# Decode attention with a partly kept K cache: keys dealt to partitions in runs of 64, K and V loaded in whole, half or quarter heads

## The chip, the cores and the metric

The kernel runs on one core of a Trainium2 chip. The metric is the device time of one execution in microseconds (us), from the runs listed below. The profile is one execution, recorded instruction by instruction; its span runs from the first instruction to the last. PE is TensorE, DVE is VectorE, ACT is ScalarE, POOL is GpSimd, SP is the engine whose queue issues the transfers. MiB are powers of two, MB and GB are powers of ten.

## The reference

Two identical rounds of decode attention and a small MLP, with one new token for each of 8 batch rows. The K and V caches are the same in both rounds.

```python
B, Sq, D = 8, 1, 512
Hq, Hkv, Sk, Dh = 32, 8, 8192, 128        # k_cache, v_cache: [8, 8, 8192, 128] bf16
F = 1792
...
q = (x @ wq).reshape(B, Sq, Hq, Dh).transpose(0, 2, 1, 3)
k = jnp.repeat(k_cache, 4, axis=1); v = jnp.repeat(v_cache, 4, axis=1)
p = _softmax(jnp.einsum("bhqd,bhkd->bhqk", q, k) * Dh ** -0.5)
o = jnp.einsum("bhqk,bhkd->bhqd", p, v) ... @ wo
...
x = x + _A_ref(_layernorm(x), A_k_cache, A_v_cache, A_wq, A_wo)
x = x + _B_ref(_layernorm(x), B_w1, B_w2)     # silu(x @ w1) @ w2
x = x + _A_ref(_layernorm(x), A_k_cache, A_v_cache, A_wq, A_wo)
x = x + _B_ref(_layernorm(x), B_w1, B_w2)
```

One K or V head of one batch row is 8192 x 128 bf16, 2 MiB. There are 64 K heads and 64 V heads, and each is wanted twice.

## The kernel before

**Tasks and positions.** The work is cut into 128 tasks: (layer, batch row, KV head). Each task has GPT = 8 groups of 1024 keys, so there are 1024 positions p, one for each iteration of the main loop (line 738). At position p the kernel emits, in this order: transposes of K up to position p + LT = p + 2 (`emit_t`, line 421), for every second position the scores of two groups (`emit_s`, line 459), and the P.V matmuls of position p - LP = p - 14 (`emit_pv`, line 523). Softmax steps of the task before, and one step of the "chain" (output projection, layer norms, MLP and next query of one batch row), are put in between. At the end of the iteration, `issue_until(p)` (line 391) issues the loads that are free to go.

**Transposes.** K arrives with keys on partitions. A group is transposed by 8 PE matmuls against the identity into PSUM (line 430), and copied back over the same place in SBUF by ACT (line 436) or DVE (line 438). V is used as it arrives.

**The arena.** K and V live in one SBUF arena of NSLOT = 27 slots of 4 KB per partition (512 KB each). Four slots hold one head. A slot is loaded by one DMA on SP's queue: key (k, p, c) of the head goes to partition p, so that a quarter head is one contiguous stretch of 512 KB in DRAM and each partition's row has 4 KB.

**What is kept.** For heads g = 3 to 7 (20 of the 32 quarters of a batch row) K, once transposed, stays in the arena from layer 0 until layer 1 of the same batch row has used it. So 88 tasks load K and V, and 40 tasks load V alone and have no transposes.

**The order of tasks** (`make_tasks`, line 138). For each batch row come, in turn:
- the *filling stage*: five layer-0 tasks with g = 3 to 7, whose K stays, so that the free part of the arena shrinks from 27 slots to 7;
- the *narrow stage*: five or six tasks with g = 0 to 2, of layer 1 of the row before and layer 0 of later rows, which run through the 7 slots left; the chain of the batch row is worked off here, and what is left of it is run at once before layer 1 begins;
- the *V-only stage*: five layer-1 tasks with g = 3 to 7, which give back the 20 slots.

The first row has three more full tasks in front, and the last three tasks stand at the end.

**The order of loads** (`plan_loads`, line 169). It works ahead of time, on positions. Each load has a position at which it is needed (`need`: K two positions before its task's group, V 14 after) and one after which its slot is free again. Loads are sorted by need; each takes the slot that came free first, and `after` is the position that freed it. At run time `issue_until(p)` issues from the front of this list while `after <= p`; a load whose `after` is larger holds back all loads behind it. The issue itself (`issue`, line 349) makes SP wait for the last readers of the slot.

```python
            def issue_until(pos):
                while queue and queue[0].after <= pos:
                    issue(queue.pop(0))
```

**The start.** Four K quarters are issued, then wq (4 MiB, rows of 8 KB), then every load with `after = -2`, which is one for each slot left, then wo, w1 and w2 (7.86 MB; rows of 1 KB, 3.5 KB and 1 KB), all on SP's queue.

Of the kernel before, what the change touches and what calls it, by code (L numbers as in the profile page):

```python
# [12 lines left out]
GRP = 8  # L13
GPT = 8
GPG = 2
NSLOT = 27
KEEP = 20
LT = 2
PRE = 10
LP = 14  # L20
EARLY = 4
# [5 lines left out]
KB = 512  # L27
QUAD = 32
FAR = 1e38
PVN = 12  # L30
# [4 lines left out]
BF16 = mybir.dt.bfloat16  # L35
# [91 lines left out]
class Load:  # L127


    __slots__ = ("kind", "b", "g", "k", "need", "free", "slot", "after")  # L130

    def __init__(self, kind, b, g, k, need, free):
        self.kind, self.b, self.g, self.k = kind, b, g, k
        self.need, self.free = need, free
        self.slot, self.after = None, None

# [31 lines left out]

def plan_loads(tasks, kept, nslot, ngran):

    at = {t: i for i, t in enumerate(tasks)}
    loads = []
    for i, (layer, b, g) in enumerate(tasks):
        for k in range(ngran):
            i0 = i * GPT + k * GPG
            if layer == 0 or (g, k) not in kept:
                need = -1 if i0 < PRE else i0 - LT
                last = i if layer or (g, k) not in kept else at[(1, b, g)]
                loads.append(Load("K", b, g, k, need, last * GPT + (k + 1) * GPG - 1))
            loads.append(Load("V", b, g, k, i0 + GPG - 1 + LP, i0 + GPG - 1 + LP))  # L180
    loads.sort(key=lambda d: (d.need, d.kind))
    free = [(-2, s) for s in range(nslot)]
    for d in loads:
        free.sort()
        d.after, d.slot = free.pop(0)
        assert d.after < d.need or d.need == -1 and d.after == -2, (d.kind, d.need, d.after)
        free.append((d.free, d.slot))
    return loads
# [18 lines left out]
def _build(ctx, nc, A_x, A_k_cache, A_v_cache, A_wq, A_wo, B_w1, B_w2, out):  # L207
# [8 lines left out]
    NGRAN = NCH // (GRP * GPG)  # L216
    SLOT = GRP * GPG * 128
    assert GPT * GRP == NCH and NGRAN * GPG == GPT and KT * 128 == D and FT * 128 == F

    order = [(g, k) for g in range(HKV) for k in range(NGRAN)]  # L220
    kept = set(order[len(order) - KEEP:])
    tasks = make_tasks(B, HKV, (len(order) - KEEP) // NGRAN)
    assert len(tasks) == 2 * B * HKV
    task_at = {t: i for i, t in enumerate(tasks)}
    loads = plan_loads(tasks, kept, NSLOT, NGRAN)
    NG = len(tasks) * GPT

# [16 lines left out]

    ARENA = sb([128, NSLOT * SLOT], BF16, "arena")

    def chunk(slot, c):
        o = slot * SLOT + c * 128
        return ARENA[:, o:o + 128]

    def half(slot, h):
        o = slot * SLOT + h * GRP * 128
        return ARENA[:, o:o + GRP * 128]

# [47 lines left out]
    syn = Sync(nc, ctx)  # L302
    slsem = [DmaCounter(syn.new_sem(f"sl{i}")) for i in range(NSLOT)]
    wsem = {n: DmaCounter(syn.new_sem(f"w_{n}")) for n in ("wq", "wo", "w1", "w2", "x")}
# [8 lines left out]

    def r_half(slot, h):
        return res(f"slot{slot}_{h}")

# [28 lines left out]

    k_slot = {}
    v_slot = {}

    def issue(d):
        cache = A_k_cache if d.kind == "K" else A_v_cache  # L350
        src = cache[d.b, d.g].rearrange("(k p c) d -> k p (c d)", k=NGRAN, p=128)[d.k]
        dst = ARENA[:, d.slot * SLOT:(d.slot + 1) * SLOT]
        dma(sp, dst, src, slsem[d.slot], writes=[r_half(d.slot, 0), r_half(d.slot, 1)])
        (k_slot if d.kind == "K" else v_slot)[(d.b, d.g, d.k)] = d.slot

    with nc.Block() as block:

        @block.sync
        def _(sync_eng):
# [42 lines left out]

            for _n in range(NGRAN):
                issue(queue.pop(0))
# [8 lines left out]
            def has_t(i):  # L413
                layer, _b, g = tasks[i // GPT]
                return layer == 0 or (g, (i % GPT) // GPG) not in kept

            def where(i):
                _l, b, g = tasks[i // GPT]
                return b, g, (i % GPT) // GPG, i % GPG

            def emit_t(i):
                b, g, k, h = where(i)
                slot = k_slot[(b, g, k)]
                n = tevacs[0]
                tevacs[0] += 1
                tb = evacs[0] % NTP
                evacs[0] += 1
                tpv = TPp[tb][:, :].rearrange("p (k q) -> p k q", q=128)
                steps = [
                    lambda c=c: pe.transpose(tpv[:, c, :], chunk(slot, h * GRP + c), ident[:, :])  # L430
                    for c in range(GRP)
                ]
                mm_group(steps, reads=[r_half(slot, h), "ident"], writes=[f"TP{tb}"])
                dst = half(slot, h)
                if n % 8 in ACT_EVAC:
                    op(act, lambda: act.copy(dst, TPp[tb][:, :]), reads=[f"TP{tb}"], writes=[r_half(slot, h)])  # L436
                else:
                    op(dve, lambda: dve.tensor_copy(dst, TPp[tb][:, :]), reads=[f"TP{tb}"], writes=[r_half(slot, h)])  # L438

# [15 lines left out]
            def emit_s(i):  # L455
                ti = i // GPT
                b, g, k, _h = where(i)
                slot = k_slot[(b, g, k)]
                bank, qn = ti % NSCP, ti % NQB
                steps = [  # L460
                    lambda c=c: pe.matmul(  # L461
                        SCp[bank][c * QUAD:(c + 1) * QUAD, :], QB[qn][:, NGRAN - 1 - k:NGRAN - 1 - k + QUAD],
                        ARENA[:, slot * SLOT + c * KB:slot * SLOT + (c + 1) * KB],
                        start=(k == 0), stop=(k == NGRAN - 1),
                    )
                    for c in range(NQ)
                ]
                mm_group(steps, reads=[r_half(slot, 0), r_half(slot, 1), f"QB{qn}"], writes=[f"SC{bank}"])

# [53 lines left out]
            def emit_pv(i):  # L523
                ti = i // GPT
                b, g, k, h = where(i)
                slot = v_slot[(b, g, k)]
                ob, pb = ti % 2, ti % NPT
                pv = PT[pb][:, :, :].rearrange("p x (c r k) -> p x c k r", c=NQ, k=NGRAN)
                otp = OTp[ob][:, 0:REP * PVN].rearrange("p (r n) -> p r n", n=PVN)
                steps = []  # L530
                for c in range(GRP):
                    cc = (i % GPT) * GRP + c
                    steps.append(
                        lambda c=c, cc=cc: pe.matmul(  # L534
                            otp, chunk(slot, h * GRP + c), pv[:, cc % CPB, cc // CPB % NQ, k, :].unsqueeze(2).to_broadcast([128, REP, PVN]),
                            start=(cc == 0), stop=(cc == NCH - 1),
                        )
                    )
                mm_group(steps, reads=[r_half(slot, h), f"PT{pb}"], writes=[f"OT{ob}"])

# [286 lines left out]
```

## Time and profile before

| | |
|---|---|
| runs | 1214.28, 1216.26, 1218.24 us; median 1216.26 |
| span of the profiled execution | 1216.1 us |
| PE busy | 1048.9 us (86%) |
| DVE, ACT, POOL busy | 598.4, 373.9, 70.3 us |
| DMA | 468.02 MB, mean 385 GB/s |
| K loads, V loads | 352 and 512, 512 KB each, median 14.9 and 10.8 us from issue to landing |
| mean granted PE clock | 0.967 |

The profiled execution's own time is not listed apart from its span; the span lies 0.2 us under the median of the runs. On the page, "DMA" gives the busy share of the 16 DMA engines in 40 equal slices of the span, in tenths, and "GB/s" what they moved in each slice. A line of the waits names the engine that waited, for whom, the total, the number of waits and the longest. In a view by stretch, each line has the busy time of each engine, the granted PE clock, the DMA share and GB/s.

### The profile page before, as it was taken

Reading aid. Unit: us, or ns where it says so; the run is one execution under the profiler, and the core shown is the slowest. Engines: PE = TensorE matmul, PEld = TensorE weight load, DVE = VectorE, ACT = ScalarE, POOL = GpSimd, SP = SyncE. Lnnn points to the kernel's source line nnn. Section 1 sums busy time; section 2 is a strip of 40 time slices with the busy share of each in tenths; the row PEclk is TensorE's granted clock in tenths of the full one; section 3 lists DMA queues with packets and bytes.
Section 4 is the critical chain, followed back from the end, with each engine's and each line's share of the span. In section 5 each row is a group of like instructions: output and inputs, shape, how many; then the busy total and the mean of one; then the engine's idle time right before and its main releaser. Section 6 shows DMA issues by size and latency. Waiting matters only on the chain.

```text
span 1216.1 us, 45620 instructions
## 1 busy us (share of the span) xinstructions
PE 1048.9 (86%) x19960; PEld 787.6 (65%) x19960; DVE 598.4 (49%) x1833; ACT 373.9 (31%) x658; POOL 70.3 (6%) x172
## 2 busy tenths in 40 slices
PE   2798888888988889889998898888988898899995
PEld 2576675667666676667676676667666666667664
DVE  2454554546445554546345654556354554456443
ACT  1233322333133322333133322332233322333231
POOL 0000000000000000000000000000000000000000
PEclk9889999999999899999879999999999999999896
DMA  9999989999999999999999999999999999999994
GB/s 373 385 397 402 393 328 409 408 400 389 365 408 409 355 343 403 408 400 388 390 408 403 383 369 409 408 399 362 376 407 402 389 370 408 408 392 380 394 407 169
DMA packets 131621, 468.02 MB, mean 385 GB/s; under 512 B 13904, under 2 KB 19808, under 8 KB 130912
## 3 DMA queue, kind: packets, MB, share of 16 engines
q1 hardware_dynamic: 131424, 465.12, 98.3%
q8 instruction: 158, 2.59, 0.8%
q14 instruction: 39, 0.32, 0.1%
HBM read 465.05 MB, written 0.01 MB: 382 GB/s over the span
## 4 chain that ended last, share of the span: by engine, by line
DMA 53%; PE 34%; SPq 5%; DVE 5%; issue 2%; POOLq 0%; POOL 0%; ACT 0%; DVEq 0%
DMA arena<-in_A_k_cache_dram 46%; PE OTp L534 11%; PE TPp L430 10%; PE SCp L461 5%; SPq L331 5%; DMA arena<-in_A_v_cache_dram 5%; PE MISC L603 4%; DMA wo<-in_A_wo_dram 2%; DVE arena L438 1%; PE OTp L482 1%; PE MISC L621 1%; PE TPp L510 1%; DVE PT L514 0%; DVE tr L585 0%; DVE yr L588 0%
## 5 line engine op out<-in xcount | busy, mean ns | idle before, releaser
L430 PE MATMUL TPp<-ident,arena 128*128 128x128 bf16 x5632 | 403.5, 223 | 80.2 <-DMA arena<-in_A_k_cache_dram 64.6
L436 ACT COPY arena<-TPp 128x1024 bf16<-128x1024 bf16 x264 | 267.2, 1012 | 603.8 <-PE TPp L430 603.8
L438 DVE COPY arena<-TPp 128x1024 bf16<-128x1024 bf16 x440 | 302.0, 688 | 279.4 <-PE TPp L430 279.1
L534 PE MATMUL OTp<-PT,arena 128*128 128x48 bf16 x8192 | 387.2, 186 | 48.1 <-DMA arena<-in_A_v_cache_dram 9.7
L534 PEld LDWEIGHTS OTp<-PT,arena 128*128 128x128 bf16 x8192 | 277.4, 97 | 226.8 <-PE OTp L534 86.1
L430 PEld LDWEIGHTS TPp<-ident,arena 128*128 128x128 bf16 x5632 | 333.8, 100 | 111.6 <-DMA arena<-in_A_k_cache_dram 92.9
L461 PE MATMUL SCp<-arena,QB 128*32 128x512 bf16 x2048 | 210.7, 401 | 7.2 <-DVE arena L438 5.4
L492 ACT ACTIVATE P<-SCp,shift 128x512 bf16<-128x512 f32 x128 | 88.4, 691 | 176.5 <-PE OTp L534 145.2
L501 POOL PARTITION_ALL_REDUCE ssa<-ssm x128 | 55.4, 433 | 998.4 <-DVE ssm L498 970.1
L514 DVE COPY PT<-TPp 128x256 bf16<-128x256 bf16 x128 | 37.3, 291 | 115.2 <-PE TPp L510 115.2
L485 DVE SCALAR_TENSOR_TENSOR own<-OTp,real,far 128x64 f32<-128x64 f32 x128 | 36.3, 284 | 112.8 <-PE OTp L482 112.4
L461 PEld LDWEIGHTS SCp<-arena,QB 128*32 128x32 bf16 x2048 | 53.2, 94 | 56.3 <-DVE arena L438 6.6
L472 DVE TENSOR_REDUCE rowmax<-SCp 128x1 f32<-128x512 f32 x128 | 86.9, 679 | 1.6 <-PE SCp L461 1.2
L482 PE MATMUL OTp<-spread,ones 128*128 128x64 f32 x256 | 52.4, 288 | 0.3 <-DVE spread L474 0.2
L510 PE MATMUL TPp<-ident,P 128*128 128x128 bf16 x512 | 50.4, 221 | 1.6 <-issue 1.6
L498 DVE TENSOR_SCALAR ssm<-hm,rs 128x4 f32<-128x4 f32 x128 | 28.5, 223 | 36.7 <-ACT P L492 36.7
L621 PE MATMUL MISC<-at,wo 128*128 128x32 bf16 (+1 forms) x1152 | 40.0, 176 | 7.1 <-DMA wo<-in_A_wo_dram 6.8
L482 PEld LDWEIGHTS OTp<-spread,ones 128*128 128x128 f32 x256 | 40.1, 198 | 0.6 <-DVE spread L474 0.6
L621 PEld LDWEIGHTS MISC<-at,wo 128*128 128x128 bf16 x1152 | 34.5, 96 | 7.5 <-DMA wo<-in_A_wo_dram 6.9
L603 PE MATMUL MISC<-xnT,wq 128*128 128x32 bf16 (+1 forms) x1152 | 34.7, 176 | 3.2 <-issue 2.8
L603 PEld LDWEIGHTS MISC<-xnT,wq 128*128 128x128 bf16 x1152 | 32.7, 97 | 3.7 <-issue 3.1
L474 DVE TENSOR_SCALAR spread<-ident,rowmax 128x64 f32<-128x64 bf16 x128 | 32.6, 254 | 4.6
(47 smaller groups left out, 293.7 us busy)
## 6 DMA issues: line engine op xcount, KB each, us to landing
arena<-in_A_v_cache_dram SPq DMA_DIRECT2D x512, 512.0 KB, 10.8
arena<-in_A_k_cache_dram SPq DMA_DIRECT2D x352, 512.0 KB, 14.9
wq<-in_A_wq_dram SPq DMA_DIRECT2D x1, 4096.0 KB, 16.5
wo<-in_A_wo_dram SPq DMA_DIRECT2D x1, 4096.0 KB, 25.9
w<-in_B_w_dram SPq DMA_DIRECT2D x2, 1792.0 KB, 22.6
P<-in_A_x_dram SPq DMA_DIRECT2D x1, 8.0 KB
out_dram<-P SPq DMA_DIRECT2D x1, 8.0 KB
```

Source lines behind the costliest of these rows:

```text
L331: eng.dma_start(out_ap, in_ap).then_inc(counter.sem, 16)
L430: lambda c=c: pe.transpose(tpv[:, c, :], chunk(slot, h * GRP + c), ident[:, :])
L436: op(act, lambda: act.copy(dst, TPp[tb][:, :]), reads=[f"TP{tb}"], writes=[r_half(slot, h)])
L438: op(dve, lambda: dve.tensor_copy(dst, TPp[tb][:, :]), reads=[f"TP{tb}"], writes=[r_half(slot, h)])
L461: lambda c=c: pe.matmul(SCp[bank][c * QUAD:(c + 1) * QUAD, :], QB[qn][:, NGRAN - 1 - k:NGRAN - 1 - k + QUAD], ARENA[:, slot * SLOT + c * K ...
L472: op(dve, lambda: dve.tensor_reduce(rowmax[:, :], SCp[bank][:, :], AX.X, ALU.max), reads=[f"SC{bank}"], writes=["rowmax"])
L482: mm_group([lambda: pe.matmul(every, ones[:, :], spread[:, :], start=True, stop=True)], reads=["ones", "spread"], writes=[f"OT{ob}"])
L492: op(act, lambda: act.activation(P[:, :], SCp[bank][:, :], ACT.Exp, bias=shift[:, 0:1], scale=SM_SCALE, accum_out=rs[st][:, :]), reads=[f" ...
L510: lambda c=c: pe.transpose(tpv[:, c, :], P[:, c * 128:(c + 1) * 128], ident[:, :])
L534: lambda c=c, cc=cc: pe.matmul(otp, chunk(slot, h * GRP + c), pv[:, cc % CPB, cc // CPB % NQ, k, :].unsqueeze(2).to_broadcast([128, REP, P ...
L603: lambda o=o, k=k: pe.matmul(MISC[:, o * n:o * n + w], w_sb[:, k, o * 128:(o + 1) * 128], rhs_of(k).to_broadcast([128, w]) if n == 1 else ...
L621: lambda o=o, h=h: pe.matmul(MISC[:, o * w:(o + 1) * w], wo_sb[:, h, o * 128:(o + 1) * 128], rhs_of(h).to_broadcast([128, w]) if n == 1 el ...
```

## The change

The arena keeps its size but is counted in 54 units of 2 KB per partition (one group of 1024 keys each) instead of 27 slots. Partition p now holds keys 64p to 64p + 63 of a head, 16 KB in one piece of DRAM. A load takes n = 8, 4 or 2 units (a whole, half or quarter head) next to each other in the arena, so that each partition's row has 16, 8 or 4 KB; a half or a quarter reads its rows from places 16 KB apart. Freeing still goes by pairs of units.

The planner first lists all quarters that are wanted, each with need and last use, sorted by need. For the first that is not yet placed it tries a whole head, then a half, then a quarter: all its parts must be still unplaced and of one kind (staying or not), and there must be a span of the arena that is free at least 16, 10 or 1 positions before the need. Among the spans that fit, a whole or half head takes the one that came free last, a quarter the one that came free first. The rest is the bookkeeping by unit. The order of PE's, DVE's, ACT's and POOL's instructions is the same as before.

```diff
-NSLOT = 27
+UPS = 2
+NUNIT = 54
 KEEP = 20
+WIDE = ((8, 16), (4, 10), (2, 1))
...
+FIRST = 4
...
+def plan_loads(tasks, kept, nunit):
     at = {t: i for i, t in enumerate(tasks)}
+    wanted = []
+    for i, (layer, b, g) in enumerate(tasks):
+        for u in range(GPT):
+            end = i * GPT + (u | 1)
+            if layer == 0 or (g, u) not in kept:
+                start = i * GPT + (u & ~1)
+                stays = layer == 0 and (g, u) in kept
+                last = at[(1, b, g)] * GPT + (u | 1) if stays else end
+                wanted.append((-1 if start < PRE else start - LT, "K", i, u, last, stays))
+            wanted.append((end + LP, "V", i, u, end + LP, False))
+    wanted.sort(key=lambda d: (d[0], d[1]))
+    of = {(d[1], d[2], d[3]): d for d in wanted}
+    free = [-2] * nunit
+    done = set()
     loads = []
...
+    for need, kind, i, u, _last, stays in wanted:
+        if (kind, i, u) in done:
+            continue
+        for n, slack in WIDE:
+            parts = [of.get((kind, i, u + x)) for x in range(n)]
+            if u % n or any(d is None or d[1:4] in done or d[5] != stays for d in parts):
+                continue
+            spans = [(max(free[s:s + n]), s) for s in range(0, nunit - n + 1, min(n, 2))]
+            fits = [x for x in spans if need - x[0] >= slack]
+            if fits:
+                break
+        after, s = max(fits) if n > 2 else min(fits)
+        for x, d in enumerate(parts):
+            done.add(d[1:4])
+            free[s + x] = d[4]
+        loads.append(Load(kind, tasks[i][1], tasks[i][2], u, n, need, s, after))
     return loads
...
     def issue(d):
         cache = A_k_cache if d.kind == "K" else A_v_cache
-        src = cache[d.b, d.g].rearrange("(k p c) d -> k p (c d)", k=NGRAN, p=128)[d.k]
-        dst = ARENA[:, d.slot * SLOT:(d.slot + 1) * SLOT]
-        dma(sp, dst, src, slsem[d.slot], writes=[r_half(d.slot, 0), r_half(d.slot, 1)])
+        src = cache[d.b, d.g].rearrange("(p c) d -> p (c d)", p=128)[:, d.u * UNIT:(d.u + d.n) * UNIT]
+        dst = ARENA[:, d.unit * UNIT:(d.unit + d.n) * UNIT]
+        dma(sp, dst, src, slsem[d.unit], writes=[r_unit(d.unit + x) for x in range(d.n)])
...
-            for _n in range(NGRAN):
+            for _n in range(FIRST):
                 issue(queue.pop(0))
...
             def emit_s(i):
...
+                units = [k_unit[(b, g, k * GPG + h)] for h in range(GPG)]
+                per = UNIT // KB
...
-                        ARENA[:, slot * SLOT + c * KB:slot * SLOT + (c + 1) * KB],
+                        whole(units[c // per])[:, c % per * KB:(c % per + 1) * KB],
```

`emit_t` and `emit_pv` take their 1024 keys from a unit instead of half a slot.

## The prediction

> **What bounds the kernel now.** I read the DMA lines of the page first, then the busy times by stretch, then the transfers of single stretches.
>
> ```profile
> DMA  9999989999999999999999999999999999999994
> GB/s 373 385 397 402 393 328 409 408 400 389 365 408 409 355 343 403 408 400 388 390 408 403 383 369 409 408 399 362 376 407 402 389 370 408 408 392 380 394 407 169
> DMA packets 131621, 468.02 MB, mean 385 GB/s; under 512 B 13904, under 2 KB 19808, under 8 KB 130912
> ...
> q1 hardware_dynamic: 131424, 465.12, 98.3%
> ```
>
> The 16 DMA engines are busy in nearly every slice, yet the rate dips from a ceiling of 408 or 409 GB/s to 328. Of the 465 MB, the 864 K and V loads are 453 MB; at 408 GB/s they alone need 1110 us of the 1216. The second view is the busy time by stretch: a V-only stage, a filling stage, a narrow stage, the wq load, part of the wo load, and a stretch at half clock (columns: PE, PEld, DVE, ACT, POOL busy, granted clock, DMA share, GB/s).
>
> ```profile
> 317.00:337.00 20.00, 18.08 (x344) 11.67 (x340) 8.03 (x33) 3.46 (x12) 1.73 (x4) 1.00 1.01 388
> 345.00:395.00 50.00, 43.96 (x787) 33.02 (x784) 25.43 (x65) 19.02 (x30) 2.15 (x5) 1.00 1.03 408
> 396.00:455.00 59.00, 50.13 (x1017) 39.73 (x1014) 31.16 (x105) 18.39 (x30) 3.75 (x9) 0.94 0.95 348
> 10.00:19.00 9.00, 2.90 (x28) 2.61 (x28) 1.49 (x8) 1.01 (x1) 0.00 (x0) 1.00 1.00 416
> 49.00:56.00 7.00, 5.45 (x104) 4.02 (x101) 3.15 (x9) 3.58 (x6) 0.43 (x1) 1.00 1.10 351
> ...
> 600.00:620.00 20.00, 19.40 (x238) 12.36 (x238) 6.12 (x23) 2.70 (x10) 1.29 (x3) 0.50 1.03 408
> ```
>
> The filling stage (second line) sits at the ceiling, 408 GB/s, with PE idle 6 of 50 us: DMA bounds it. In the narrow stage (third) the rate falls to 348 while PE works 85% of the time with the chain of the MLP in between: PE and its dependences bound it, and only 7 of 27 slots move. The transfers of the arena say the same, first for the filling stage, then for the narrow one:
>
> ```profile
> DMA to landing us min/median/max: 8.1/15.2/16.1
> ```
>
> ```profile
> DMA to landing us min/median/max: 3.9/6.5/9.3
> ```
>
> 15.2 us at 408 GB/s is 6.2 MB queued, about 12 loads; 6.5 us is about 5. So the change pays where the ceiling is reached (filling and V-only stages) and should leave the narrow stage as it is.
>
> **Part 1: longer rows.** Going through the new planner's loop with this kernel's task list gives 51 whole heads, 136 halves and 388 quarters, 575 loads for 864; the bytes are the same. Nearly all quarters lie in the narrow stages. What a row costs comes from two lines above. wo has rows of 1 KB and ran at 351 GB/s: 16 x 1024 B / 351 = 46.7 ns a row on each engine. K and V have 4 KB rows at 408: 160.6 ns. The difference, 113.9 ns for 3072 B, is 37.1 ps a byte, which leaves 8.7 ns for each row whatever its length. So 8 KB takes 312.6 ns (419 GB/s) and 16 KB 616 ns (425 GB/s). The only 8 KB rows in the trace are those of wq, at 416 GB/s, beside the line's 419. Bounds: at least nothing (408), at most no fixed cost (16 / 37.1 ps = 431). I take the line, since the wq row is near it. A half head then takes 2.503 instead of 2.570 us, 136 x 0.067 = 9.2 us; a whole one 4.930 instead of 5.140, 51 x 0.210 = 10.7 us. **Together -19.9 us**, between 0 and -32.6 (all 249.6 MB at 431).
>
> The Trainium skill (DMA: Bandwidth & Descriptors, Where 436 GB/s comes from) sets the ceiling by the SBUF ports at 435 GB/s; the trace's 408 lies below it. Were all wide loads at 435, the gain would be 38 us.
>
> Does PE let the gain through? In the filling stage PE is busy 43.96 of 50 us, 9.0 of the 10.2 us of a task; a task's 4.19 MB would take 9.9 us, still more. In the V-only stage the window 317:337 holds 256 P.V matmuls (line 534), 8 to a position: 32 positions in 20 us, 0.62 us each, for 262 KB: PE takes 423 GB/s, about what halves give (419).
>
> **Part 2: quarters out of rows 16 KB apart.** A quarter was one stretch of 512 KB; now it is 128 pieces of 4 KB, one in every 16 KB. The trace has no such load of K or V. Nearest rows: wq, whose 8 KB rows lie 1 MiB apart within a partition, reached the highest rate of all, and wo's 1 KB rows, 128 KB apart within a partition, fit the line. I take nothing; the bounds are 0 and a rival below.
>
> **Part 3: loads issued later.** Before, a load takes the slot that came free first; the data issued but not yet needed grows from 2.5 MiB in the narrow stage to 12 MiB by the end of the V-only stage. The new planner takes, for a wide load, the span that came free last among those with 16 (whole) or 10 (half) positions to spare. SP issues in order, so a late one holds back all behind it; going through the list, this lead is now 2 to 10 MiB outside the narrow stages (1 at one place), and 2.5 in them as before. As the queue is what keeps DMA at 408, I asked at each load: if PE stands waiting for it, how much is issued behind it, and how long does PE need from there to release the next? A lone 512 KB load landed after 3.7 us, of which its bytes are 1.3: 2.4 us is fixed. In the V-only stage a half is issued 10 positions ahead, 6.2 us; it needs 2.4 + 2.5 = 4.9. The queue never runs dry but at one place: position 255 waits for a whole V head with only 1 MiB (2.5 us) behind it, and the next issue is 3 positions and 2.4 us away, 4.3 us. **+1.8 us.** Where PE waits for a whole K and a whole V at once, it waits longer and then has 8 positions without a wait; DMA works on, so this costs nothing while loads stand behind.
>
> **Part 4: start and end.** Ahead of wo, w1 and w2 now stand 10 MiB of K and V instead of 13.5, so the weights come some 9 us sooner and the 6.8 us in which PE waits for wo go; what is late next is the whole V head for position 23, which lands behind them. DMA has work throughout, so the order costs nothing. At the end the last V load is a whole head. Now only the last quarter's matmuls follow the last landing:
>
> ```profile
> 1200.84 0.37 PEld L534 LDWEIGHTS OTp<-PT,arena 128*128 128x128 bf16 x8 [0.26 <-DMA arena<-in_A_v_cache_dram]
> 1200.88 1.04 PE L534 MATMUL OTp<-PT,arena 128*128 128x48 bf16 x16
> 1201.41 0.37 PEld L534 LDWEIGHTS OTp<-PT,arena 128*128 128x128 bf16 x8 [0.19 <-PE OTp L534]
> 1201.95 0.17 DVE L548 TENSOR_TENSOR at<-OTp,rcp 128x4 bf16<-128x4 f32 x1 [4.75 <-PE OTp L534]
> ```
>
> 16 matmuls in 1.04 us; 64 will follow then, 4.2 us: **+3.1 us.** The 27 more semaphores and the 289 DMA instructions that go are on SP, which waits anyway (14 us of the 50 in the filling stage for line 534), so they count nothing. PE, DVE and ACT issue the same instructions.
>
> **Sum.** 1216.1 - 19.9 + 1.8 + 3.1 = 1201.1 us. The span (1216.1) is 0.2 under the median of the three runs (1216.26), so the forecast is **1201**.
>
> **Rivals.**
> 1. *The thinner lead starves DMA* (slower). Price: the V-only stage from 317 to 337 us begins on a queue not yet filled and moved 388 GB/s. If the queue stays that thin, the 83.9 MB of wide loads needed in V-only stages (46 halves, 17 wholes) go at 388, 10.6 us more than at 408, and those of the filling stages gain nothing: 1216.1 + 10.6 + 4.9 = 1232. It decides as soon as a half head needs over 6.2 us from release to landing in the V-only stage, 1.3 us more than I count. For it: the half-clock stretch at 600 us fell into a V-only stage, and the old lead kept DMA at 408 there. With 238 PE matmuls for 344, a position takes 0.90 us, V loads that follow PE move 291 GB/s, and such a stretch would lose 5.7 us. Against it: the margins of part 3. Chance 0.14.
> 2. *Quarters slow down by their gaps* (slower). 388 loads; break-even is 15 us / 388 = 39 ns each, 3% of 1.285 us. At 5%, +25 us: 1226. Against it: wq. Chance 0.08. The Trainium skill (DMA: Bandwidth & Descriptors, Latency and other measured facts) has copies at a row pitch of 512 KiB at 207 GB/s where a padded pitch gave 214, and at 4 MiB at 103. Its smallest loss, 3%, on the quarters would be 17 us, 1218; 16 KiB is under its range, and wq's steps of 1 MiB at 416 GB/s do not show it.
> 3. *No change*: PE, fed in lumps of whole heads, needs its 9.0 us a task plus gaps that waiting now hides, and the filling stages stay at 10.2 us. They hold most of the saving (86 halves and 25 wholes, 11 us): 1201 + 11 = 1212, and with a half-clock stretch 1217. Chance 0.13.
> 4. *Long rows cost nothing extra* (431 GB/s): -32.6 + 4.9 = 1188. Chance 0.12.
>
> **How the numbers follow.** The forecast has 0.53 (1194 to 1209). Faster by over 0.3% (3.6 us, what a measurement here can tell from no change): the forecast, rival 4 and a little of rival 3, 0.67. Within 0.3%: 0.11. Slower: rivals 1 and 2, 0.22. The range, 1189 to 1229, leaves out the ends of rivals 1, 2 and 4.
>
> **What would show it.** In the page after: GB/s of the best slices 415 to 425, not 408; about 41,600 fewer packets if a row stays one packet (36,992 rows, and 16 small ones for each of 289 loads); 575 issues. Filling tasks at 9.9 us, V-only ones still at 4.95, the narrow stage unchanged with landings near 6.5 us. If best slices stay at 408, part 1 is wrong; if narrow stages get slower at full DMA share, rival 2 holds; if DMA share falls under 1.0 in V-only or filling stages, rival 1 does. Wrong altogether would be a PE that cannot take 9.9 us a task.

## The result, and the profile after

The change made the kernel slower: 1269.39 us (median of 4 runs, 1264.32 to 1276.72) against 1217.25 us for the kernel before, run beside it (4 runs, 1214.28 to 1221.05). The ratio is 1.044, with a 95% interval of 1.040 to 1.049. The forecast was 1201, the range ended at 1229. The profiled execution has a span of 1270.3 us, 54.2 more than before.

The page's second part shows both halves of the story: what was hoped for, and what came with it.

```profile
DMA  9999999999899999999999999999999999999992
GB/s 373 382 410 384 378 357 375 387 359 373 309 429 385 364 335 391 386 354 360 337 413 365 365 343 397 397 373 357 349 422 384 373 363 400 413 357 364 352 428 92
DMA packets 90000, 467.95 MB, mean 368 GB/s; under 512 B 9281, under 2 KB 15185, under 8 KB 65361
...
q1 hardware_dynamic: 89808, 465.10, 94.7%
```

The queue has 41,616 packets fewer (forecast 41,600), and the best slices reach 422 to 429 GB/s, where the ceiling was 408. Yet the mean fell from 385 to 368, and the queue's share from 98.3% to 94.7% of a longer span. So DMA had cheaper work and did it less of the time.

Windows of the changed kernel (columns as in the prediction: PE, PEld, DVE, ACT, POOL busy, granted clock, DMA share, GB/s): one V-only stage, the end of the filling stage after it, the narrow stage after that, and 4 us inside the V-only stage.

```profile
325.00:361.00 36.00, 32.18 (x466) 20.65 (x462) 10.70 (x42) 5.34 (x16) 2.16 (x5) 0.67 0.93 354
376.00:409.00 33.00, 32.03 (x625) 25.39 (x622) 18.81 (x49) 15.22 (x24) 1.72 (x4) 1.00 0.99 408
410.00:467.00 57.00, 48.93 (x1021) 38.64 (x1018) 31.18 (x105) 18.30 (x30) 3.75 (x9) 0.97 0.94 346
341.00:345.00 4.00, 3.74 (x48) 1.99 (x44) 1.44 (x6) 0.00 (x0) 0.43 (x1) 0.50 0.45 123
```

The V-only stage moved 354 GB/s (388 in the window of before) and ran two thirds of full clock. In its worst 4 us DMA was busy 45%.

**One load, followed.** A V half needed at position 247 was released by position 237, ten before it, as the prediction counts. It was issued at 328.6 us with 1 MiB still ahead of it and landed at 336.2: 7.6 us, where the prediction had 4.9 and PE needs 6.2 for ten positions. It is no exception: of the 44 V halves needed in V-only stages 37 took over 6.2 us, and the page has this median for all 103 V halves, in all stages:

```profile
arena<-in_A_v_cache_dram SPq DMA_DIRECT2D x103, 1024.0 KB, 7.9
```

The timeline shows PE stopping from 334.1 to 336.25; its clock is at half from 335.3 to 359.2:

```profile
333.68 0.40 PE L480 MATMUL SCp<-arena,QB 128*32 128x512 bf16 x4
...
336.25 0.94 PE L553 MATMUL OTp<-PT,arena 128*128 128x48 bf16 x13 [2.17 <-DMA arena<-in_A_v_cache_dram]
```

A few positions later stands the whole head that the prediction named as the one dry place (position 255). SP's waits in 325:361 have it:

```profile
SPq L92 <- PE OTp L553: 23.6, 6, 10.4
SPq L348 <- PE OTp L553: 4.2, 3, 2.7
```

From 332.0 to 342.4 us SP waited for the P.V matmuls of position 253 to give back a span. DMA first worked off what had been issued; the 123 GB/s above is where that ran out. So the stop of PE costs DMA nothing at once, it makes the next loads later. The half clock adds to it: the eight positions up to 253 took 6.2 us (336.25 to 342.4), and at the 0.62 us each of the kernel before they would have taken 5.0, an estimate. Before, SP's waits for P.V in 317:345 were short:

```profile
SPq L331 <- PE OTp L534: 5.8, 8, 1.2
```

**Where the 54 us came from.** I split every execution in two: *rows* is the time the 16 DMA engines need for all packets of SP's queue at full speed (in this trace a 16 KB row takes 611 ns, 8 KB 309, 4 KB 159, by the median), and *lost* is the rest of the span, in which DMA stood or worked more slowly. A stage runs from the first score matmul of its first task to that of the next stage. The times and ratios are medians, against runs of before beside them (1215.32 to 1217.25); one execution each of e9 and e14 was over 1.5% slower than the fastest of its kernel and is left out. The rest is us from one profiled execution each, which lies up to 8 us off the median (e2's 8 above, e14's 5 above, e6's 6 below):

| kernel | median, ratio to before (95%) | rows | lost | V-only | filling | narrow | start and end |
|---|---|---|---|---|---|---|---|
| before | 1217.25 | 1142.0 | 74.1 | 5.3 | 2.9 | 44.7 | 21.3 |
| changed | 1269.39, 1.044 (1.040 to 1.049) | 1117.5 | 152.9 | 35.8 | 22.1 | 65.9 | 29.0 |
| e1 | 1231.17, 1.012 (1.008 to 1.016) | 1142.0 | 90.9 | 8.0 | 3.0 | 57.8 | 22.1 |
| e2 | 1245.07, 1.025 (1.021 to 1.029) | 1116.7 | 134.7 | 11.0 | 19.6 | 75.8 | 28.2 |
| e3 | 1266.00, 1.042 (1.039 to 1.046) | 1142.0 | 124.6 | 44.4 | 1.8 | 57.3 | 20.9 |
| e4 | 1221.97, 1.006 (1.003 to 1.009) | 1126.7 | 89.9 | 7.4 | 4.8 | 53.6 | 24.0 |
| e5 | 1212.84, 0.999 (0.996 to 1.001) | 1128.1 | 80.2 | 9.9 | 4.9 | 44.3 | 21.0 |
| e6 | 1226.48, 1.010 (1.006 to 1.014) | 1142.0 | 76.5 | 5.9 | 5.9 | 42.2 | 22.5 |
| e7 | 1291.32, 1.063 (1.060 to 1.067) | 1117.5 | 167.7 | 35.5 | 33.1 | 70.8 | 28.4 |
| e8 | 1263.85, 1.042 (1.039 to 1.044) | 1116.7 | 147.2 | 8.3 | 33.4 | 75.6 | 29.9 |
| e9 | 1228.80, 1.009 (1.006 to 1.012) | 1120.0 | 110.0 | 14.5 | 17.0 | 56.9 | 21.7 |
| e10 | 1225.39, 1.007 (1.004 to 1.009) | 1119.4 | 107.3 | 6.4 | 17.2 | 62.0 | 21.6 |
| e11 | 1215.68, 0.999 (0.997 to 1.001) | 1134.1 | 77.3 | 9.9 | 4.1 | 41.5 | 21.7 |
| e12 | 1219.17, 1.003 (1.001 to 1.005) | 1123.1 | 93.4 | 8.3 | 9.3 | 54.3 | 21.5 |
| e13 | 1243.14, 1.021 (1.016 to 1.026) | 1120.0 | 118.5 | 18.5 | 15.2 | 62.1 | 22.6 |
| e14 | 1237.84, 1.015 (1.008 to 1.022) | 1142.0 | 99.3 | 32.0 | 2.5 | 44.4 | 20.5 |
| e15 | 1223.64, 1.006 (1.003 to 1.008) | 1126.0 | 97.2 | 7.4 | 5.6 | 60.2 | 23.9 |

The rows cost 24.5 us less. The lost time grew by 78.8: V-only +30.5, filling +19.2, narrow +21.2, start and end +7.7. The net is +54.3, the difference of the spans but for rounding. The V-only loss is in every one of the eight stages, 3.7 to 6.0 us each; before, it was 0.1 to 1.2.

### The profile page after: what moved, and what is told of

Its sections match the earlier page's. It is cut to its first block, busy times and chain, and to the rows that moved or that the text cites. A ratio compares the mean times of both kernels' runs of the same rounds, so it can differ in the third digit from the quotient of the medians.

```text
span 1270.3 us, 44750 instructions
## 1 busy us (share of the span) xinstructions
PE 1077.8 (85%) x19960; PEld 811.5 (64%) x19960; DVE 600.0 (47%) x1833; ACT 373.8 (29%) x658; POOL 70.3 (6%) x172
## 3 DMA queue, kind: packets, MB, share of 16 engines
q1 hardware_dynamic: 89808, 465.10, 94.7%
## 4 chain that ended last, share of the span: by engine, by line
PE 50%; DMA 41%; issue 4%; DVE 4%; SPq 1%; POOL 0%; POOLq 0%; ACT 0%; DVEq 0%
DMA arena<-in_A_v_cache_dram 26%; PE OTp L553 17%; PE TPp L447 16%; DMA arena<-in_A_k_cache_dram 15%; PE SCp L480 8%; PE MISC L622 4%; PE MISC L640 2%; PE OTp L501 2%; PE TPp L529 1%; DVE arena L455 1%; SPq L348 1%; DVE tr L605 0%; DVE tr L604 0%; DVE yr L607 0%; DVE PT L533 0%
## 5 line engine op out<-in xcount | busy, mean ns | idle before, releaser
L553 PE MATMUL OTp<-PT,arena 128*128 128x48 bf16 x8192 | 408.9, 191 | 107.9 <-DMA arena<-in_A_v_cache_dram 72.3
L553 PEld LDWEIGHTS OTp<-PT,arena 128*128 128x128 bf16 x8192 | 294.4, 100 | 306.5 <-PE OTp L553 109.7
L447 PE MATMUL TPp<-ident,arena 128*128 128x128 bf16 x5632 | 411.1, 225 | 54.2 <-DMA arena<-in_A_k_cache_dram 36.9
L447 PEld LDWEIGHTS TPp<-ident,arena 128*128 128x128 bf16 x5632 | 344.5, 102 | 68.8 <-DMA arena<-in_A_k_cache_dram 48.2
L480 PE MATMUL SCp<-arena,QB 128*32 128x512 bf16 x2048 | 227.3, 434 | 5.3 <-DVE arena L455 3.4
L480 PEld LDWEIGHTS SCp<-arena,QB 128*32 128x32 bf16 x2048 | 53.6, 95 | 58.2 <-issue 7.5
L501 PE MATMUL OTp<-spread,ones 128*128 128x64 f32 x256 | 56.5, 306 | 0.7 <-issue 0.4
L529 PE MATMUL TPp<-ident,P 128*128 128x128 bf16 x512 | 54.9, 236 | 0.0
L501 PEld LDWEIGHTS OTp<-spread,ones 128*128 128x128 f32 x256 | 43.6, 214 | 1.0 <-DVE spread L493 0.5
## 6 DMA issues: line engine op xcount, KB each, us to landing
arena<-in_A_v_cache_dram SPq DMA_DIRECT2D x25, 2048.0 KB, 15.2
```

The source lines that it names most:

```text
L447: lambda c=c: pe.transpose(tpv[:, c, :], chunk(unit, c), ident[:, :])
L480: lambda c=c: pe.matmul(SCp[bank][c * QUAD:(c + 1) * QUAD, :], QB[qn][:, NGRAN - 1 - k:NGRAN - 1 - k + QUAD], whole(units[c // per])[:, c ...
L501: mm_group([lambda: pe.matmul(every, ones[:, :], spread[:, :], start=True, stop=True)], reads=["ones", "spread"], writes=[f"OT{ob}"])
L529: lambda c=c: pe.transpose(tpv[:, c, :], P[:, c * 128:(c + 1) * 128], ident[:, :])
L553: lambda c=c, cc=cc: pe.matmul(otp, chunk(unit, c), pv[:, cc % CPB, cc // CPB % NQ, k, :].unsqueeze(2).to_broadcast([128, REP, PVN]), star ...
```

## The experiments

Four causes could make DMA lose time: **the lead** (loads issued later, so that the queue runs thin and PE arrives before its data); **the gaps** (rows of a quarter 16 KB apart); **the clock** (PE halved by a stall, theory T); **the lumps** (whole heads, which a stage must wait for in one piece). Short diffs are against the changed kernel unless another is named; all kernels compute the whole reference.

**e1: the gaps alone.** Quarters only, each in the span that came free first. This is the plan of before with the new dealing.

```diff
-WIDE = ((8, 16), (4, 10), (2, 1))
+WIDE = ((2, 1),)
...
-        after, s = max(fits) if n > 2 else min(fits)
+        after, s = min(fits)
```

> The changed kernel with quarters alone, each in the span that came free first: the new deal of keys and rows 16 KB apart stay, the order and the time of the loads are those of before. Theory A (wide loads are issued too late: PE waits in the V-only stages, the clock falls to half, and loads that follow PE slow down): as before, 1217 us, V-only stages 233 us in all, half clock some 80 us. Theory B (lumps: PE must wait for 1 or 2 MiB to land at once): the same 1217. Theory C (rows 16 KB apart are slow): narrow stages 10 us longer than before or more, and as every load is now such a quarter, 25 us or more over before, 1240.

Measured 1231.17, 14.8 us over before, so the gaps cost something by themselves, though less than theory C had. That it is not the counting by units is shown by e14 and e5 below: their quarters in the narrow stages are contiguous, and the narrow stages lose what they lost before. A filling stage of e1:

```profile
350.00:400.00 50.00, 43.55 (x762) 33.06 (x762) 24.37 (x62) 19.14 (x30) 2.15 (x5) 0.97 1.03 408
```

The same narrow stage, before and in e1, the one with the largest difference of the eight:

```profile
534.60:587.60 53.00, 47.77 (x1007) 37.57 (x1006) 31.57 (x106) 18.30 (x30) 3.75 (x9) 1.00 1.01 385
539.90:597.90 58.00, 50.25 (x1007) 39.47 (x1006) 31.59 (x106) 18.42 (x30) 3.76 (x9) 0.94 0.96 351
```

With a full queue a gapped quarter is as fast as a contiguous one: 408 GB/s, as before. It is the landing of a load with little ahead of it that is later. The very first load, alone on the queue, in e1, and then before:

```profile
DMA to landing us min/median/max: 4.1/4.1/4.1
...
DMA to landing us min/median/max: 3.7/3.7/3.7
```

Over all traces this load takes 4.0 to 4.4 us in the nine kernels where it is gapped and 3.7 to 3.95 in the eight where it is not. With four loads ahead the medians are 6.4 (e1) and 6.1 (before), with eleven both 15.2. The ledger puts 13 of the 17 us in the narrow stages, where the queue is short.

**e2: the lead alone.** The change, with every load in the span that came free first (61 whole heads, 118 halves, 384 quarters).

```diff
-        after, s = max(fits) if n > 2 else min(fits)
+        after, s = min(fits)
```

> The changed kernel, but a wide load too takes the span that came free first: 61 whole heads, 118 halves, 384 quarters, much as in the changed kernel, while the data issued ahead in the V-only stages is 6.0 MiB in the mean instead of 4.0 (8.2 before). Theory A: most of the loss goes, half clock falls from 271 us towards 80, V-only stages from 302 towards 235 us, time 1200 to 1225. Theory B: PE still waits for the same lumps, so the time stays at 1255 to 1270. Theory C: 1255 to 1270 too.

Measured 1245.07, between theories A and B: 23 of the changed kernel's 52 us go. The V-only loss falls from 35.8 to 11.0; the filling (19.6) and narrow (75.8) losses stay. The half-clock time did not fall as theory A had it: 232 us in all, of 271.

**e3: late quarters.** As e1, but a quarter with ten positions to spare takes the span that came free last.

```diff
-WIDE = ((8, 16), (4, 10), (2, 1))
+WIDE = ((2, 10), (2, 1))
...
-        after, s = max(fits) if n > 2 else min(fits)
+        after, s = max(fits) if slack > 1 else min(fits)
```

> Quarters alone, but outside the narrow stages each takes the span that came free last among those with 10 positions to spare: no wide load and no lump, but as little lead as in the changed kernel (V-only stages: 3.0 MiB issued ahead in the mean, where the changed kernel has 4.0 and before 8.2). Theory A: the loss is there without any wide row, 1245 to 1290 us, V-only stages 270 to 320 us, half clock over 180 us. Theory B: no lumps, so no loss, 1217 to 1225. Theory C: as the quarters with early issue.

Measured 1266.00, nearly the changed kernel's time without one wide load, as theory A had it. So wide loads are not needed for a loss of that size. e3's V-only stage, and its SP waits there:

```profile
327.00:360.00 33.00, 29.86 (x454) 19.48 (x451) 10.66 (x40) 5.35 (x16) 2.17 (x5) 0.74 0.90 328
```

```profile
SPq L92 <- PE OTp L553: 21.6, 17, 2.3
```

**e14: late quarters without gaps.** The plan of e3, with the contiguous quarters of before.

```diff
-        src = cache[d.b, d.g].rearrange("(p c) d -> p (c d)", p=128)[:, d.u * UNIT:(d.u + d.n) * UNIT]
+        src = cache[d.b, d.g].rearrange("(k p c) d -> k p (c d)", k=NGRAN, p=128)[d.u // GPG]
```

> Contiguous quarters as before the change, but issued late as in the quarters with 10 positions to spare (1266 us with rows 16 KB apart). Theory A with separate costs: late issue costs the same 35 us that it cost on quarters with gaps, 1216 + 35 = 1251. If the gaps cost more where the lead is short, because the landing time is what the short lead runs on: 1225 to 1243.

Measured 1237.84, in the second range. This closes a square: neither 1217, gaps +14.8, lateness +21.1, both +49.6. Each costs time alone; together they cost some 14 us more than the sum, not far over the 11 us that the three intervals, taken together, leave in doubt. The V-only loss of e14 (32.0) comes from lateness alone, and the narrow stages, whose quarters are contiguous as before, lose nothing more (44.4).

**e15: more positions to spare.** The change with 24 and 16 positions instead of 16 and 10; the plan then has 4 whole heads, 169 halves and 510 quarters.

```diff
-WIDE = ((8, 16), (4, 10), (2, 1))
+WIDE = ((8, 24), (4, 16), (2, 1))
```

> The changed kernel with 24 and 16 positions to spare instead of 16 and 10, the choice of the span that came free last kept: 4 whole heads, 169 halves, 510 quarters, and at least 3.5 MiB ahead everywhere in the V-only stages (1.0 in the change), 5.4 in the mean. Theory A: the V-only stages fall from 302 to 245 us or less, the time to 1222 to 1238. If the rule that takes the span freed last does harm by itself, whatever is to spare: 1245 or more.

Measured 1223.64, as theory A had it: 45 of the 52 us gone, with late issue and gaps still in (the V-only stages take 260 us, not the 245 expected). V-only and filling stage of e15:

```profile
317.00:348.00 31.00, 28.29 (x451) 18.52 (x448) 10.11 (x40) 5.34 (x16) 2.17 (x5) 0.78 1.01 410
357.00:395.00 38.00, 33.66 (x640) 25.95 (x639) 20.53 (x52) 15.22 (x24) 1.73 (x4) 1.00 1.02 414
```

DMA is full in both (410 and 414 GB/s), and their losses are 7.4 and 5.6. Since the plan also has hardly a whole head left, e15 alone does not part the lead from the lumps. For the V-only stages e2 (whole heads, early), e13 (whole heads, more lead) and e14 (no whole heads, late) do.

**e13 and e9: no wide loads for heads 0 to 2.** These heads' loads stand in and just behind the narrow stages, where a wide one needs many of the few free units. e13:

```diff
         for n, slack in WIDE:
+            if n > 2 and tasks[i][2] < 3:
+                continue
```

> The plan of the changed kernel with the deal by head (heads 0 to 2 in quarters alone, late issue for the wide loads of the others: 53 whole heads, 103 halves, 446 quarters), but all heads dealt in runs of 64 as in the change, so that the quarters of heads 0 to 2 have rows 16 KB apart again. That deal by head took 1231 us, the changed kernel 1269. If the gaps are the whole difference: 1262 to 1272. If it is the plan (no wide loads of heads 0 to 2, 4.9 MiB instead of 4.0 ahead in the V-only stages): 1231 to 1238. If the early quarters' 15 us carry over and the plan makes the rest: 1243 to 1252.

e9 in addition deals these heads to partitions by the quarter, so that all their loads are contiguous:

```diff
+        per = 2 if d.g < 3 else 8
+        src = cache[d.b, d.g].rearrange("(h p c) d -> h p (c d)", h=GPT // per, p=128)[d.u // per]
+        src = src[:, d.u % per * UNIT:(d.u % per + d.n) * UNIT]
```

> The changed kernel with its late issue and its wide loads, but heads 0 to 2 are dealt as before the change and loaded in contiguous quarters alone; heads 3 to 7 as in the change. 53 whole heads, 103 halves, 446 quarters. Theory C (rows 16 KB apart slow the quarters of the narrow stages): narrow stages fall from 469 us to 455 to 462, time from 1269 to 1250 to 1258; V-only stages stay near 295 to 305 us. If the loss of the narrow stages comes from the late issue or the lumps, they stay at 465 to 470 us and the time at 1262 to 1272.

Measured 1243.14, in the third range, and 1228.80, under both of e9's ranges: 26 us for leaving out the wide loads of three heads, 14 more for the gaps alone. Of the first step 17 us show in the V-only stages (35.8 to 18.5). It changes the whole plan: more whole V heads are needed in the V-only stages than in the changed kernel (17 for 11), but 4.9 MiB stay issued ahead there in the mean for 4.0, and at least 2.0 for 1.0. So there it is the lead that counts, not the lumps.

**e10: e9 with early issue**, `after, s = min(fits)` throughout.

> The same deal by head, and every load in the span that came free first: 54 whole heads, 106 halves, 436 quarters, 6.1 MiB ahead in the V-only stages. With neither late issue nor gaps in the narrow stages, what is left is the lumps and the shorter lead that whole heads need. Theory B (lumps cost): 1225 to 1240, though the rows are 23 us cheaper than before. If lumps cost nothing: 1216 less 23, 1190 to 1200.

Measured 1225.39, as theory B had it. The rows cost 22.6 us less than before, and 33 are lost again: 17.2 in filling and 62.0 in narrow stages. The filling loss of 15 to 22 us is in each kernel with 50 or more whole heads at 16 positions to spare, early or late (changed, e2, e9, e10, e13; 33 in e7 and e8, whose columns slow PE); in those without it is under 10.

**e4, e5, e11, e12: halves only, early.** e4 has halves with 18 positions to spare; e5 is e4 with heads 0 to 2 in contiguous quarters and the others dealt in two contiguous halves (`per = 2 if d.g < 3 else 4`, and no half for heads 0 to 2); e11 is e5 with halves in layer 0 alone; e12 is e5 with 10 positions.

```diff
-WIDE = ((8, 16), (4, 10), (2, 1))
+WIDE = ((4, 18), (2, 1))
...
-        after, s = max(fits) if n > 2 else min(fits)
+        after, s = min(fits)
```

> No whole heads; a half only where a span is free 18 positions ahead, in the span that came free first: 172 halves and 520 quarters, 7.1 MiB issued ahead in the V-only stages. Theory A: no loss, and the halves gain 0.067 us each, 11.5 us in all: 1205. Theory B: smaller lumps, half the loss or less, 1225 to 1240. Theory C: near the quarters with early issue.

> The halves of 18 positions again, but the deal of keys is chosen by head. Heads 0 to 2, which fill the narrow stages, are dealt as before the change: quarters of one contiguous 512 KB, never wider. Heads 3 to 7 are dealt in two halves of one contiguous 1 MB each, rows of 8 KB; their quarters have 4 KB rows 8 KB apart. 156 halves, 552 quarters, 7.2 MiB ahead in the V-only stages. Theory C (rows 16 KB apart cost the 14 us by which the early quarters stood over before, most of it in the narrow stages): narrow stages go back from 465 to 459 us, the filling stages stay at 392, time 1200 to 1209, under both kernels. If the 14 us had another cause (the counting by units, the longer list of semaphores), 1218 to 1224 as with the halves before.

> Deal by head with halves of contiguous 1 MB, 18 positions ahead, only for layer 0 of heads 3 to 7: 89 halves, 686 quarters, and the V-only stages have quarters again, 7.8 MiB ahead. By rows: 89 x 0.067 = 6 us under before, 1210. If the V-only stages with halves (248 us against 233) were what ate the gain of the halves, V-only falls to 233 to 238 and the time lies at 1206 to 1212; if not, 1212 to 1218.

> Deal by head, halves of contiguous 1 MB with 10 positions instead of 18 to spare, the span that came free first: 212 halves, 440 quarters, 7.1 MiB ahead in the V-only stages as with 18. By rows 212 x 0.067 = 14 us, 3.8 us better than with 18. Theory B with lumps of 1 MB: more halves, more waits, 1215 to 1225. If only whole heads are too large a lump: 1205 to 1212.

Measured 1221.97, 1212.84, 1215.68 and 1219.17. e4 and e5 fell into none of their ranges, e11 into the one in which halves in V-only stages are not what eats the gain, e12 into that of 1 MB lumps. From e4 to e5 the gaps and the halves of heads 0 to 2 go together, and the narrow stages lose 44.3 again instead of 53.6. e5 saves 13.9 us of rows, and its median is 2.5 us under before, with 1 inside the interval of the ratio: neither e5 nor e11 can be told from the kernel before. e12 has the most halves (212) and the fewest positions to spare of the four; its rows cost 18.9 us less, its lost time is 19.3 more.

**e6: the clock alone.** The kernel before, with one pause of PE in each V-only stage: 16 small GpSimd writes to a scratch tile, for which PE waits (it stands 4.3 us).

```diff
+                if p in lulls:
+                    last = [res(f"OT{(p - LP) // GPT % 2}")]
+                    for _n in range(16):
+                        tok = op(pool, lambda: pool.memset(LULL[:, :], 0.0), reads=last, writes=["LULL"])
+                    syn.wait(pe, tok)
```

> The kernel before, with one pause of PE in each V-only stage, at its twelfth position: PE waits for 16 memsets of GpSimd on a scratch tile, some 3.5 us; nothing else changes, and the lead of the loads is the long one. Theory T (clock trap: after an idle time of some 2 us in a V-only stage the clock falls to half and stays there until the transposes of the filling stage come): half clock from 82 to some 220 us or more, V-only tasks of 7.1 us behind the pause, V-only stages 233 to some 290 us; with the long lead DMA stays near 400 GB/s and the filling stages, with their data there, run at 8.7 us a task and give much back: 1220 to 1240. If the half clock has another cause than the pause (more DMA traffic, wide rows): half clock stays near 82 us, V-only stages grow by the 28 us of the pauses at most.

Measured 1226.48, as theory T had it. V-only stage and filling stage of e6:

```profile
326.00:354.00 28.00, 25.90 (x328) 16.45 (x329) 7.50 (x28) 3.61 (x10) 2.67 (x9) 0.52 1.03 410
355.00:397.00 42.00, 40.80 (x791) 32.37 (x788) 25.33 (x65) 19.02 (x30) 2.15 (x5) 1.00 1.02 402
```

The V-only stages ran 167 us at half clock (27 before). They took 64.2 us more (233.0 to 297.2), the filling stages 50.7 less. DMA ran on at 410 GB/s, since its loads were released long before, and PE found the data waiting. A slow PE costs little as long as the loads do not wait for it: 11 us by the medians, pauses included. e14 has the same half clock in this V-only stage, with late loads:

```profile
324.00:355.00 31.00, 29.97 (x380) 18.49 (x381) 8.86 (x34) 3.97 (x15) 2.17 (x5) 0.50 0.87 309
```

309 GB/s against 410: the lead makes the difference, and with a short one a slow PE slows DMA.

**e7 and e8: the clock kept up.** Each P.V matmul gets 80 columns instead of 48 (every weight repeated 20 times instead of 12; one copy is used), in the changed kernel (e7) and in e2 (e8).

```diff
-PVN = 12
+PVN = 20
```

> The changed kernel with 20 instead of 12 copies of each P column in the P.V matmuls, 80 columns instead of 48; the copies are not used, so only PE's activity changes. Theory T: the busier V-only stage lets the clock come back before the stage ends, half clock falls from 271 us to 150 or less, V-only stages from 302 to 270 or less, time 1240 to 1258; the late issue still costs the rest. If the low clock is only a result of waiting for data (theory A alone), the V-only stages stay at 295 to 310 us and the time at 1265 to 1285.

> The wide loads issued early (1245 us, V-only stages 280 us, 150 of them at half clock), with the same 80 columns. Theory T: here the data is there, so that the clock is all that is left: half clock in the V-only stages falls to 60 us or less, the stages to 245, the time to 1220 to 1232. If lumps cost by themselves (theory B), 1240 to 1255.

Measured 1291.32 and 1263.85, over all the ranges. In e7 the half-clock time in V-only stages falls from 186 to 52 us, and DMA still loses 35.5 us there (35.8 in the changed kernel). One V-only stage of e7:

```profile
330.00:367.00 37.00, 31.11 (x460) 21.04 (x457) 10.19 (x40) 5.34 (x16) 2.16 (x5) 0.86 0.89 344
```

DMA's share is below 0.9 at a clock of 0.86. Half-clock time and loss do not go together over the kernels: in the V-only stages they are 186 and 35.8 us in the changed kernel, 52 and 35.5 in e7, 90 and 32.0 in e14, but 150 and 11.0 in e2 and 167 and 5.9 in e6. So theory T falls as the main cause: the late loads lose DMA time with little half clock, and early ones keep it with much. The columns themselves add 0.7 us to a V-only task at full clock (4.95 to 5.64) and as much to a filling task, where e7 and e8 lose 33 us; for that reason e8, meant for the lumps, decides nothing.

## Why the prediction was wrong, step by step

- **Part 1 (rows) held.** Forecast 616, 312.6 and 160.6 ns a row, measured 611, 309 and 159; -19.9 us forecast, -24.5 in the ledger (2.6 of it are the 4,624 small packets that went, 9 ns each on 16 engines, which the sum left out). PE lets it through too: the last filling tasks take 8.7 us, under the 9.0 I feared and the 10.2 of before, and the filling stages are 30.7 us shorter in sum (408.9 to 378.2). Rival 3 fell.
- **Part 3 (loads later) failed**, and with it the forecast. The sentence at fault is "it needs 2.4 + 2.5 = 4.9". It takes a half as alone on the queue, right after I had written that a queue stands behind it; the same queue stands ahead of it. With 1 MiB ahead, 2.5 us by the prediction's own rate, the sum would have been 7.4 against 6.2 available; 7.6 was measured. So "The queue never runs dry but at one place" was wrong too: every V-only stage lost 3.7 to 6.0 us, with 4.0 MiB issued ahead there in the mean, for 8.2 before. That is rival 1, at the point I gave for it ("over 6.2 us from release to landing"), and it decides whole stages. Rival 1's price, 16 us, was too low as well: it let the rate fall to 388 GB/s, but once PE stands, a load follows PE and PE follows the load, and the stage went at 354. Lateness alone costs 21 us (e14; the changed kernel less e2 gives 23), and with 24 and 16 positions the V-only loss is 7.4 us, near the 5.3 of before (e15).
- **The dry place** at position 255 was the right one, and its price was near: 1.8 us forecast, and the 4 us at a DMA share of 0.45 are 2.2 us lost. What was wrong is that it was held to be the only one. In e13, where the plan has two halves there instead of the whole head, this stage loses 2.5 us instead of 6.0.
- **Part 2 (gaps) failed in size.** "I take nothing" held for the rate at a full queue and not for the landing: 0.4 us more for a lone load, 14.8 us in all (e1). wq, which I set against it, was read behind a full queue and could not show this. So rival 2 had the wrong mechanism (the rows are no slower at a full queue). That the gaps of e1's 864 quarters took the 15 us that it named as the break-even for 388 is chance.
- **Lumps were put at nothing.** "This costs nothing while loads stand behind" does not fit the filling stages: their 19 us more of lost time go with whole heads at 16 positions to spare. Rival 3 looked for the price of lumps on PE; what goes with them here is DMA's time.
- **Part 4.** At the start the wait for wo went, and the wait for the whole V head came in its place, as said, 14.3 us instead of 6.8; the loss of DMA there is 0.6 us. At the end the last V load landed at 1247.7, and this is the timeline just before the last normalisation:

```profile
1254.94 0.37 PEld L553 LDWEIGHTS OTp<-PT,arena 128*128 128x128 bf16 x8 [0.19 <-PE OTp L553]
1255.50 0.37 PEld L553 LDWEIGHTS OTp<-PT,arena 128*128 128x128 bf16 x8 [0.19 <-PE OTp L553]
1256.05 0.17 DVE L567 TENSOR_TENSOR at<-OTp,rcp 128x4 bf16<-128x4 f32 x1 [4.10 <-PE OTp L553]
```

  8.3 us lie between, 1.3 before: some 120 P.V matmuls were still to do, not 64, as PE had only just begun the head before. +3.1 forecast, +7.0 measured.
- **Narrow stages** were to stay as they were, and lose 21.2 us more. About 13 of it is the gaps, if they cost as much as in e1; what makes the rest is not shown. The kernels with many whole heads all lose more there than e5, e11 and e14, which have none and contiguous quarters.

What stays open: the lumps, the shorter lead that whole heads leave, and the clock are not parted in the filling stages, since no kernel was run in which whole heads keep a lead as long as before's. Why a gapped quarter lands 0.4 us later is not shown; only that its rate at a full queue is the same. How much the half clock itself adds to the changed kernel's time was not measured, because e7's columns cost time of their own; that it adds some is seen in the one stage followed above.

## What to carry to other kernels

Price a load from release to landing with everything that stands ahead of it in its queue, and set that against the time its consumer needs for the positions in between; a plan that looks one load at a time misses it. Longer rows were worth 2% here, but they were paid for with lead, with gaps where the queue is thin, and, as it seems, with pieces that must land whole. When a change buys rate, count for each stage how many bytes stay issued ahead, before and after.

## What the runs showed of the hardware

- **Row cost** is close to a straight line: 46.7 ns for 1 KB (wo, by its rate), 159 for 4 KB, 309 for 8 KB, 611 for 16 KB (by the median). The 1 and 4 KB rows of the kernel before leave 8.7 ns a row that do not depend on its length, and the longer rows fit that; of 159 ns this is under 6%, the most that rows over 4 KB could gain by it.
- **Gaps between rows** do not lower the rate at a full queue (408 GB/s in e1 and before) but delay a landing on a short one (4.1 against 3.7 us alone, 6.4 against 6.1 with four loads ahead).
- **The clock** fell 1.2 us into a stop of PE of 2.2 us and stayed at half for 23.9 us (335.3 to 359.2 in the changed kernel), though PE was busy for 19.9 of the 20.8 us after the stop, up to the first transposes of K at 357.0. In e6 seven of the eight pauses of 4.3 us brought it down, 1.1 to 4.0 us after PE stopped; in the eighth stage it was at half already. In four of e6's stages it came back 2.6 to 2.8 us after the first transposes of K, in the other four within the stage, after 10 to 17 us at half. The Trainium skill (TensorE: Matmul & The Clock Gate, Part 1: The HAM clock gate) has the clock fall after an idle window of about 3.4 us and return after as long a busy one; here a shorter stop was enough, and busy time in a V-only stage brought it back late or not at all. With 80 columns instead of 48 the half-clock time in V-only stages was 52 us for 186.
